# Global filter plus product-key experts on one core: leftover rows in 64 by 64 pieces stacked by DMA, guards from sums of squares, and a new order

## The chip, the cores and the metric

The kernel runs on one core of one Trainium2 chip. The metric is the device time of one execution in microseconds (us). Names of the engines: PE multiplies matrices, DVE is the vector engine, ACT the scalar engine, POOL the GpSimd engine, SP the sync engine, which here only issues transfers.

## The reference, cut to what matters

```python
x: (1, 2048, 576);  xn = layernorm(x)
# spectral part
y = irfft2(rfft2(xn) * (w_r + 1j * w_i))                 # over 2048 and 576
# experts: 32 heads, two halves of 128, 8 keys each
q = einsum("nd,dhc->nhc", xn, w_q)                       # w_q (576, 32, 256)
i1 = argmax(q[..., :128] @ k1.T);  i2 = argmax(q[..., 128:] @ k2.T)
e  = i1 * 8 + i2                                         # one expert per head, gate 1
act = gelu(xn . u[e])                                    # u, v (64, 576)
out = x + y + sum over heads of act * v[e]
```

## The kernel before, in words

The 2048 tokens lie in 16 tiles of 128. Everything is one program whose operations are recorded and then issued in an order that a table of numbers, `ORDER`, writes out by hand; a second table, `BANK`, says which PSUM banks each result takes (`_Plan.issue`, line 305). So every recorded instruction has line 312 in the profile, and groups are told apart by their tiles. Each engine takes its instructions in that order and never passes one by. All transfers are issued by SP, one queue in order. At most eight of them are under way, since their completions turn over eight semaphores.

**Spectral part.** `folds` (509) makes of each token tile the even and odd halves of a row; `dft128` (525) transforms along the sequence in 64-point pieces on halves of PE (64 rows by 128 columns). Of the 161 columns of a half, 128 go into the main store `AB` as an fp16 value and an fp16 remainder, by ACT and DVE. The 33 that are left over go into `ABL`, 99 partitions high: value, value, remainder, stacked. To get them there, `folds` copies the 33 columns three times side by side (`fl`, on ACT or POOL), four matmuls write 99 rows at once, and two evictions (ACT 99 by 256, DVE 33 by 256) end in the right rows. `d_fwd` (785) transforms along the features: per group two matmuls from `ABL`, twelve from `AB`. `s_fwd` (801) and `s_inv` (838) are the second stage along the sequence and its inverse, in fp32 on quarters and halves of PE; `s_mul` (820) between them multiplies with the filter `Wt` (two DVE instructions with results `t`, two on POOL that make `y`). `s_inv` also has four matmuls for the leftover rows, from three copies `yl` that ACT makes. `d_inv` (866) goes back along the features, and `fin` (895) along the sequence. Sixteen groups g pass `d_fwd`, `s_fwd`, `s_mul`, `s_inv`; then sixteen tiles pass `d_inv` and `fin`. The first `d_inv` needs `AB` and `ABL` of all sixteen groups.

**Experts.** `fold_part` (626) reads w_q in 32 loads `w` of 576 KB (five buffers) and multiplies each with differences of the keys (`KP`, four matmuls); the result becomes the matrix `MU` (`fold_end`, `fold_last`). `x_t` (694) loads the transposed tokens `xf` and splits them into `xT`. `scores` (708) multiplies `MU` with `xT` (28 matmuls of 128 by 512 per pair of tiles) and takes maxima over seven differences; `route` (734) turns them into codes with one reduce over seven, and one-hot rows; `combine` (754) sums them into `CAT`. In `fin` eight matmuls per pair of tiles multiply `CAT` with `vS` (fp16 value and remainder of v).

**Guards.** Before a value is split into fp16 it is scaled by its largest magnitude: a maximum per partition, then `allmax` (444): PE transpose, DVE reduce, PE matmul, DVE scaling.

Of the kernel before, what the change touches and what calls it, by code (L numbers as in the profile page):

```python
# [10 lines left out]
F32 = mybir.dt.float32  # L11
# [28 lines left out]
def _consts():  # L40
# [10 lines left out]
    place = [8 * (g % 2) + g // 2 for g in range(16)]  # L51
# [4 lines left out]
    RT = np.concatenate([R.reshape(64, 64).T] * 2)  # L56
# [42 lines left out]
    ev = ll % 2 == 0  # L99
    i = np.arange(127, -1, -1)[:, None]  # L100
    mid = _columns()[:33, None]
    half = np.where(i == 0, 0.5, 1.0)
    C1, S1 = (f(pi2 * (i * ll % 576) / 576) * half for f in (np.cos, np.sin))
    C2, S2 = (f(pi2 * (mid * ll % 576) / 576) for f in (np.cos, np.sin))
# [11 lines left out]
    for b, (m, k) in enumerate(((C1, C2), (S1, S2))):  # L116
        for q, h in enumerate(_hl(_clean(m))):
            dc[:, b, q] = h
        hi, lo = _hl(_clean(k))
        dl[:99, b] = np.concatenate([hi, hi, lo])  # L120
    for b, m in enumerate((_clean(CI) * 64, _clean(SI) * 64)):
        hi, lo = _hl(m)
        for q, h in enumerate((hi, lo)):
            ce = slice(0, 145) if b == 0 else slice(145, 290)
            co = slice(145, 290) if b == 0 else slice(0, 145)
            ic[:, b, q, ce] = h[:128, ce]
            ic[:, b, q, co] = h[161:, co]
        il[:99, b] = np.concatenate([hi[128:161], hi[128:161], lo[128:161]])
# [90 lines left out]
class _Ps:  # L219
# [9 lines left out]
    def rearrange(self, *p, **kw):  # L229
        return _Ps(self.ap.rearrange(*p, **kw), self.tile)  # L230
# [797 lines left out]
```

## Time and profile before

| | us |
|---|---|
| three runs | 207.41, 208.88, 209.98; median 208.88 |
| the profiled execution, its own time | 209.11 |
| its span | 206.3 |
| outside the span | 2.8 |
| PE busy | 195.5 (95%) |
| DVE busy | 172.8 (84%) |
| ACT busy | 120.7 (59%) |
| POOL busy | 97.6 (47%) |
| moved by DMA | 43.39 MB, mean 210 GB/s |

The profile is that of one execution. The chain of waits is followed back from the last instruction. In the timeline a row is a run of like instructions: start, length until the last has ended, engine, operation, output and inputs, tile, count; in square brackets behind it stands how long the engine had been idle and what released it. Since matmuls overlap, the cost of a run of them is the distance between its start and the next row's start. A row of the windows gives the length of a stretch, the busy time of PE, its weight loads, DVE, ACT and POOL with the counts of instructions, then the granted PE clock, the mean busy share of the 16 DMA engines and GB/s.

### The profile page before, as it was taken

How to read it: one execution, taken by the hardware profiler on the slowest of the kernel's cores; microseconds unless marked ns; L12 is line 12 of the kernel's file. 1: busy time of each engine (PE TensorE's matmuls, PEld its weight loads, DVE VectorE, ACT ScalarE, POOL GpSimd, SP SyncE). 2: the span in 40 equal slices, each digit the busy share in tenths (PEclk: the TensorE clock that was granted, in tenths of full speed). 3: DMA queues.
4: the chain of work that ended last, by engine and by line, in shares of the span. 5: the costliest groups of instructions: out<-in, count | busy, mean ns of one | idle time of the engine just before them, and what ended most of it. 6: DMA issues, size and time to landing. Idle time of an engine off the chain costs nothing.

```text
span 206.3 us, 5748 instructions
## 1 busy us (share of the span) xinstructions
PE 195.5 (95%) x2239; PEld 134.3 (65%) x2239; DVE 172.8 (84%) x397; ACT 120.7 (59%) x272; POOL 97.6 (47%) x160
## 2 busy tenths in 40 slices
PE   7588999999998999999999999999999999999992
PEld 2388669786567658544556668565686667868850
DVE  2899898847485787659999999999999999999863
ACT  2799997842437629988686936608682432333400
POOL 4548464002250033179538227405176666959750
PEclk9999999999999999999999999999999999999999
DMA  6999899999999999554725502520000000123195
GB/s 209 394 416 420 308 381 412 403 407 374 376 380 410 335 371 318 176 178 129 280 67 174 211 0 79 165 102 5 0 3 0 0 3 0 62 114 118 65 362 206
DMA packets 14859, 43.39 MB, mean 210 GB/s; under 512 B 1904, under 2 KB 4720, under 8 KB 14576
## 3 DMA queue, kind: packets, MB, share of 16 engines
q1 hardware_dynamic: 14832, 43.03, 56.6%
q8 instruction: 17, 0.28, 0.6%
q14 instruction: 10, 0.08, 0.1%
HBM read 38.30 MB, written 4.72 MB: 209 GB/s over the span
## 4 chain that ended last, share of the span: by engine, by line
PE 84%; DMA 8%; DVE 4%; ACT 1%; issue 1%; POOL 1%; DVEq 0%; SPq 0%; ACTq 0%
PE banks L312 84%; DMA w<-in_wq_dram 6%; DVE A L312 2%; DMA XN<-in_x_dram 1%; DVE st L312 1%; DVE rr L312 1%; ACT t L312 0%; POOL A L312 0%; DVE AB L312 0%; POOL MUL L312 0%; DVE XN L312 0%; ACT rr L312 0%; POOL rr L312 0%; DVEq L1022 0%; ACT yl L312 0%
## 5 line engine op out<-in xcount | busy, mean ns | idle before, releaser
L312 PE MATMUL banks<-MU,xT 128*128 128x512 f16 x192 | 46.3, 379 | 0.0
L312 POOL TENSOR_TENSOR y<-t,t 128x289 f32<-128x289 f32 x32 | 21.5, 695 | 43.8 <-DVE t L312 21.6
L312 PEld LDWEIGHTS <-AB 128*128 128x128 f16 x400 | 33.9, 122 | 6.2 <-issue 1.9
L312 PEld LDWEIGHTS <-xT 128*128 128x128 f16 x224 | 21.3, 100 | 22.8 <-issue 0.9
L312 PE MATMUL banks<-c,AB 128*128 128x145 f16 (+1 forms) x384 | 35.1, 227 | 0.0
L312 POOL TENSOR_TENSOR xT<-xf,xT 128x640 f16<-128x640 f32 x16 | 22.8, 1433 | 24.4 <-DVE w L312 10.4
L312 DVE SCALAR_TENSOR_TENSOR t<-banks,wx,Wt 128x578 f32<-128x578 f32 x32 | 24.4, 812 | 7.1 <-PE banks L312 4.1
L312 POOL TENSOR_TENSOR A<-t 128x289 f32<-128x289 f32 x32 | 21.5, 694 | 7.0 <-DVE MT L312 3.8
L312 DVE TENSOR_TENSOR AB<-banks,AB 128x512 f16<-128x512 f32 x32 | 21.2, 675 | 1.8 <-ACT AB L312 1.7
L312 PE MATMUL banks<-Rs,A 64*128 64x128 f32 x256 | 18.6, 288 | 3.9 <-ACT Rs L312 2.9
L312 ACT ACTIVATE es<-banks,sc 128x290 f32<-128x290 f32 (+1 forms) x16 | 9.9, 625 | 18.9 <-PE banks L312 12.5
L312 PEld LDWEIGHTS banks<-Rs,A 64*128 64x128 f32 x256 | 16.5, 194 | 6.3 <-ACT Rs L312 4.6
L312 PE MATMUL banks<-w,KP 128*32 128x288 f32 x256 | 18.6, 412 | 1.3 <-DMA w<-in_wq_dram 1.2
L312 ACT ACTIVATE AB<-banks 128x512 f16<-128x512 f32 x32 | 18.4, 591 | 1.7 <-PE banks L312 1.2
L312 PE MATMUL banks<-c,ABL 99*128 99x289 f16 (+1 forms) x64 | 18.5, 290 | 0.0
L312 DVE TENSOR_REDUCE MT<-w 128x128 bf16<-128x896 bf16 (+1 forms) x16 | 18.2, 1140 | 0.1
L312 ACT ACTIVATE A<-banks 128x578 f32<-128x578 f32 x16 | 10.3, 645 | 13.1 <-PE banks L312 12.2
L312 PE MATMUL banks<-A,s 64*64 64x289 f32 x256 | 17.8, 410 | 0.0
L312 PE MATMUL banks<-s,y 64*128 64x128 f32 x256 | 17.4, 278 | 0.0
L312 ACT ACTIVATE ABL<-banks 99x256 f16<-99x256 f32 x32 | 11.6, 379 | 9.3 <-PE banks L312 8.8
L312 PEld LDWEIGHTS banks<-s,y 64*128 64x128 f32 x256 | 15.4, 187 | 2.1 <-issue 1.4
L312 DVE SCALAR_TENSOR_TENSOR XN<-banks,sc,XN 128x578 f32<-128x578 f32 (+1 forms) x18 | 12.9, 746 | 1.9 <-PE banks L312 1.9
(124 smaller groups left out, 359.9 us busy)
## 6 DMA issues: line engine op xcount, KB each, us to landing
w<-in_wq_dram SPq DMA_DIRECT2D x32, 576.0 KB, 6.9
xf<-in_xT_dram SPq DMA_DIRECT2D x16, 320.0 KB, 3.3
Wt<-in_W_dram SPq DMA_DIRECT2D x8, 578.0 KB, 6.6
out_dram<-XN SPq DMA_DIRECT2D x14, 288.0 KB, 2.4
s<-in_s_dram SPq DMA_DIRECT2D x16, 192.0 KB, 5.7
XN<-in_x_dram SPq DMA_DIRECT2D x2, 1156.0 KB, 12.6
XN<-in_x_dram SPq DMA_DIRECT2D x3, 578.0 KB, 5.8
c<-in_c_dram SPq DMA_DIRECT2D x1, 868.5 KB, 11.2
```

Of the source, the lines that this page charges most:

```text
L312: o.last = fn(*[x.place() if isinstance(x, _Ps) else x for x in args], **{k: x.place() if isinstance(x, _Ps) else x for k, x in kw.items()})
```

## The change

1. **Leftover rows.** `folds` makes no copies and lays the 33 and the 31 leftover columns next to each other. (Odd halves have 31 that are not zero, so there are 64 in all.) `dft128` multiplies them with one matmul on each half of PE, 65 rows by 64, where there were two. ACT and DVE evict 64 partitions by 128 into a plain store `HL` (a view of a new tile `U`). Once all sixteen tiles are through, a new step `spread` copies `HL` into the stacked `ABL` by six transfers from SBUF to SBUF, 33 or 31 partitions of 4096 bytes each.
2. **The same on the way back.** `s_inv` keeps its eight main matmuls. A new `s_left` handles the leftover rows of two groups at once, by eight matmuls on 64 by 64 quarters; ACT and DVE evict (128 by 256 each), then six transfers of 33 partitions by 4 runs of 128 bytes stack them in `ABL`. The copies `yl` are gone.
3. `d_fwd` and `d_inv` issue the `ABL` matmuls after the `AB` ones, and these may stand apart.
4. **Guards** are roots of sums of squares: ACT squares and sums, one matmul sums over partitions, DVE takes a root by an integer operation on the bits. Ten of eleven `allmax` are replaced (`root`); five large DVE reduces over w_q's fold and two over u and v become six ACT instructions. The ACT squares of the fold write into the last `w` buffer.
5. **Remainder of v** in `fin`: four full matmuls and four on halves, two at a time, instead of eight full ones.
6. **Maximum of the codes** in `route`: three elementwise maxima over halves (2 by 192, 2 by 128, 128 elements) instead of one reduce over 896. The columns of `MU` are ordered for that.
7. **Order.** `place`, `ORDER` and `BANK` are new. Four `xf` loads and the masks `mk` now stand ahead of the last `w` load. There are 157 transfers, 103 before.

The SP queue around the new copies. Before (`w_120` to `w_119` are buffers of the w_q loads, `Wt_113<-in_v` brings v):

```order
L312 DMA c_72<-in_c_dram 128x3474
L312 DMA s_2_116<-in_s_dram 128x384
L312 DMA s_0_114<-in_s_dram 128x384
L312 DMA s_1_115<-in_s_dram 128x384
L312 DMA w_120<-in_wq_dram 128x1152
L312 DMA w_122<-in_wq_dram 128x1152
```

After, `ABL<-U` being the copies of `spread`:

```order
L322 DMA w_120<-in_wq_dram 128x1152
L322 DMA w_116<-in_wq_dram 128x1152
L322 DMA xf_121<-in_xT_dram 128x640
L322 DMA s_1_113<-in_s_dram 128x384
L322 DMA w_117<-in_wq_dram 128x1152
L322 DMA ABL<-U 31x2048
L322 DMA ABL<-U 33x2048
...
L322 DMA w_119<-in_wq_dram 128x1152
L322 DMA w_118<-in_wq_dram 128x1152
L322 DMA w_120<-in_wq_dram 128x1152
```

The 31 and 33 rows come three times in turn. Twelve of the 32 `w` loads stand ahead of the copies, twenty behind them.

PE between the last second-stage step and the first `d_inv`. Before (`s,y` and `s,yl` are `s_inv`, `MU` are scores, `c,ABL` the first `d_inv`):

```order
L312 MATMUL banks<-s_0_114,y_132 128x128 x8
L312 MATMUL banks<-s_0_114,yl_104 99x128 x4
L312 MATMUL banks<-s_1_115,y_133 128x128 x8
L312 MATMUL banks<-s_1_115,yl_105 99x128 x4
L312 MATMUL banks<-s_2_116,y_132 128x128 x8
L312 MATMUL banks<-s_2_116,yl_103 99x128 x4
L312 MATMUL banks<-s_3_117,y_133 128x128 x8
L312 MATMUL banks<-s_3_117,yl_104 99x128 x4
L312 LDWEIGHTS xT_92
L312 MATMUL banks<-MU,xT_92 128x512
...
L312 LDWEIGHTS ABL
L312 MATMUL banks<-c_72,ABL 128x290
```

After (`U` now holds `y`, `id` is a transpose of the experts' coefficients, `c,AB` the first `d_inv`):

```order
L322 MATMUL banks<-s_0_112,U 128x128 x8
L322 MATMUL banks<-s_1_113,U 128x128 x8
L322 MATMUL banks<-s_2_114,U 64x128 x2
...
L322 MATMUL banks<-s_2_114,U 128x128 x8
L322 MATMUL banks<-s_3_115,U 128x128 x8
L322 LDWEIGHTS MT
L322 MATMUL banks<-id_108,MT 128x128
...
L322 LDWEIGHTS AB
L322 MATMUL banks<-c_72,AB 128x145
```

The sixteen score matmuls that stood between the last `s_inv` and the first `d_inv` now stand earlier.

DVE in the same place, after; the four `t` are the last `s_mul`, `lo` the leftover evictions, `AB` the main ones, the others are experts:

```order
L322 SCALAR_TENSOR_TENSOR t_0_104<-banks,wx,Wt_111 128x578
L322 TENSOR_TENSOR lo_130<-banks,lo_130 128x256
L322 TENSOR_REDUCE MT<-w_119 128x32
L322 TENSOR_TENSOR AB<-banks,AB 128x16x32 x2
L322 TENSOR_TENSOR w_120<-w_120,wt 128x896
...
L322 TENSOR_TENSOR w_120<-w_120 128x2x192
L322 TENSOR_TENSOR lo_131<-banks,lo_131 128x256
L322 TENSOR_TENSOR w_120<-w_120 128x2x128
L322 TENSOR_TENSOR AB<-banks,AB 128x16x32
```

One more `AB` eviction follows four small instructions later, and the first `d_inv` waits for it.

The diff's core:

```diff
-    place = [8 * (g % 2) + g // 2 for g in range(16)]
+    place = [4 * (g % 4) + g // 4 for g in range(16)]
...
 ORDER = (
-    19, 20, 21, 22, 0, 25, 26, 11, 27, 30, 31, 23, 426, 28, 14, 39, 29, 3, 32, 33, 40, 42, 47, 46, 8, 2, 1, 4,
+    24, 19, 20, 21, 29, 27, 28, 11, 0, 22, 23, 39, 31, 30, 32, 34, 3, 47, 35, 36, 46, 2, 1, 5, 9, 4, 6, 8, 402,
...
+    def root(src, k, dst, e):
+        p = PS("m", (128, 64))
+        P.matmul(p[:, :k], on[:, 0:1].to_broadcast([128, 128]), src, start=True, stop=True)
+        v = p[:, :k].bitcast(I32)
...
+        V.tensor_scalar(dst.bitcast(I32), v, 0.5, float(0x1FBD1DF5 + (e << 23)), op0=OP.mult, op1=OP.add)
...
     def dft128(t):
-        for b in range(2):
-            for h, r in enumerate(hs):
-                P.matmul(p[:99, h, 256 + 64 * b:320 + 64 * b], fl[r, b], Rs[r, 0], start=True,
-                         stop=True, tile_position=(64 * h, 0))
+        for h, r in enumerate(hs):
+            P.matmul(p[:65, h, 256:320], e[r, 256:321], Rs[r, 0], start=True, stop=True, tile_position=(64 * h, 0))
...
-        A.activation(lo[:99], l[:99], AF.Copy)
-        V.tensor_tensor(lo[:33], l[:33], lo[:33], op=OP.subtract)
+        A.activation(lh, l, AF.Copy)
+        V.tensor_tensor(ll, l, lh, op=OP.subtract)
+
+    @staged
+    def spread():
+        for k, q in enumerate((0, 0, 1)):
+            for b, n in enumerate((33, 31)):
+                Q.dma_start(ABL[n * k:n * k + n, b], HL[31 * (1 - b):31 * (1 - b) + n, q])
...
     def fold_part(b, s):
-            if (b, s) == (3, 3):
-                V.tensor_reduce(mm_[:, 3 + h:4 + h], mt[b][:, h, :288], axis=AX, op=OP.max, apply_absolute_value=True)
...
+            A.activation(w[:, 0:2], mt[b][:, :, :288], AF.Square, accum_out=mm_[:, b:b + 1])
...
     def route(r):
-        V.tensor_reduce(v0, wv, axis=AX, op=OP.max)
+        V.tensor_tensor(wv[:, :, 4:7], wv[:, :, 4:7], wv[:, :, 0:3], op=OP.max)
+        V.tensor_tensor(wv[:, :, 3:5], wv[:, :, 3:5], wv[:, :, 5:7], op=OP.max)
+        V.tensor_tensor(v0.rearrange("p (t m) -> p t m", t=2), wv[:, :, 3], wv[:, :, 4], op=OP.max)
...
+    @staged
+    def s_left(g):
+        p = PS("c")
+        for ri in range(2):
+            for q in range(2):
+                y, s = Y[g + q], S32[g + q][:, 192:]
+                for e in range(2):
+                    r, o = slice(64 * e, 64 * e + 64), 64 * (e ^ q)
+                    P.matmul(p[o:o + 64, q, :128], y[r, ri, 128:192], s[r, 64 * ri:64 * ri + 128], start=(ri == 0),
+                             stop=(ri == 1), tile_position=(64 * e, o))
...
+        A.activation(hi, pv, AF.Copy)
+        V.tensor_tensor(lo, pv, hi, op=OP.subtract)
+        for k, n in enumerate((0, 0, 1)):
+            for e in range(2):
+                to = ABL[33 * k:33 * k + 33].rearrange("p b (a e n) -> p (b a) e n", a=2, e=2)
+                Q.dma_start(to[:, :, e, 32 * g:32 * g + 64], h[64 * e:64 * e + 33, n])
...
     def fin(t, ys):
+        for h in range(2):
+            for i in range(2):
+                r = slice(64 * i, 64 * i + 64)
+                P.matmul(ps[i][:, h, :L], CAT[r, t + i, :], vS[r, 1, L * h:L * h + L], start=False, stop=False,
+                         tile_position=(64 * i, 0))
...
-                for q in range(2):
-                    P.matmul(ps[i][:, h, :L], CAT[:, t + i, :], vS[:, q, L * h:L * h + L], start=False, stop=(q == 1))
+                P.matmul(ps[i][:, h, :L], CAT[:, t + i, :], vS[:, 0, L * h:L * h + L], start=False, stop=True)
...
     dft128(15)
+    spread()
```

More of the change, by code (lines that the diff above doesn't have):

```diff
@@ L101, in _consts @@
     mid = _columns()[:33, None]
-    half = np.where(i == 0, 0.5, 1.0)
-    C1, S1 = (f(pi2 * (i * ll % 576) / 576) * half for f in (np.cos, np.sin))
-    C2, S2 = (f(pi2 * (mid * ll % 576) / 576) for f in (np.cos, np.sin))
+    C1 = np.cos(pi2 * (i * ll % 576) / 576) * np.where(i == 0, 0.5, 1.0)
+    S1 = np.sin(pi2 * ((i + 1) * ll % 576) / 576)
+    C2, S2 = np.cos(pi2 * (mid * ll % 576) / 576), np.sin(pi2 * (mid[:31] * ll % 576) / 576)
     eps = np.where((ll == 0) | (ll == 288), 1.0, 2.0)[:, None]
@@ L270, in __init__ @@
     def __init__(self, nc):
-        self.ops, self.stage, self.pack, self.made, self.tiles = [], 0, set(), 0, []
+        self.names = {}
+        self.ops, self.stage, self.pack, self.made, self.tiles, self.split = [], 0, set(), 0, [], False
         self.engines = [_Engine(self, n, getattr(nc, n)) for n in ("vector", "scalar", "gpsimd", "tensor", "sync")]
@@ L289, in add @@
         last = self.ops[-1] if self.ops else None
-        if (eng == "tensor" and last is not None and last.eng == eng and last.stage == self.stage
+        if (eng == "tensor" and last is not None and last.eng == eng and not self.split and last.stage == self.stage
                 and last.cols + cols < 2160 and (last.tiles == tiles or last.tiles | tiles <= self.pack)):
@@ L303, in add, with cut @@
             v.users.add(len(self.ops) - 1)
+    def cut(self):
+        self.split = True
     def issue(self, tc):
@@ L403, in _body @@
     ABL = K([128, 2, S], F16, "ABL")
+    U = K([128, 2316], F32, "U")
+    slots["y"], slots["es"] = ([U[:, 579 * i:579 * i + 578] for i in range(4)], [U[:, 580 * i:580 * i + 580] for i in range(2)])
+    turn["y"] = turn["es"] = 0
+    HL = view(U, [64, 2, S], F16)
     ABg = AB.rearrange("p q c (g n) -> p q c g n", g=16)
     ABLg = ABL.rearrange("p b (g n) -> p b g n", g=16)
-    place = [8 * (g % 2) + g // 2 for g in range(16)]
+    place = [4 * (g % 4) + g // 4 for g in range(16)]
     ABt = AB.rearrange("p q c (n t) -> p q c n t", t=16)
     ABLt = ABL.rearrange("p b (n t) -> p b n t", t=16)
-    ABi = AB.rearrange("p q c (a g e m) -> p q (c a) g e m", a=2, g=16, e=2)
-    ABLi = ABL.rearrange("p b (a g e m) -> p (b a) g e m", a=2, g=16, e=2)
+    ABi = AB.rearrange("p q c (a e g m) -> p q (c a) g e m", a=2, g=16, e=2)
     wu = AB[:, 0, 0, 0:512]
@@ L439, in g @@
             plan.stage += 1
+            plan.names[plan.stage] = (f.__name__, *(x for x in args if isinstance(x, int)))
             return f(*args)
@@ L563, in uv_prep @@
         Q.dma_start(vs, a["v2"])
-        V.tensor_reduce(uv[:, 0:1], uf, axis=AX, op=OP.max, apply_absolute_value=True)
-        V.tensor_reduce(uv[:, 1:2], vs, axis=AX, op=OP.max, apply_absolute_value=True)
-        allmax(uv[:, 0:2], 2, sc[:, 0:2])
+        for k, z in enumerate((uf, vs)):
+            A.activation(vS[:, 0, :z.shape[1]], z, AF.Square, accum_out=uv[:, k:k + 1])
+        root(uv[:, 0:2], 2, sc[:, 0:2], 1)
+        V.tensor_scalar(sc[:, 0:2], sc[:, 0:2], 1e-10, None, op0=OP.max)
         V.reciprocal(sc[:, 4:6], sc[:, 0:2])
@@ L787, in d_fwd @@
         for b in range(2):
-            P.matmul(p[:, b, :L], ABLg[:99, b, place[g], :], dl[:99, b, :], start=True, stop=False)
             for c in range(2):
@@ L791, in d_fwd @@
                 for n, (ha, hb) in enumerate(((0, 0), (0, 1), (1, 0))):
-                    P.matmul(p[:, b, cs], ABg[:, ha, 2 * b + c, place[g], :], dc[:, b, hb, cs], start=False,
-                             stop=(c == 1 and n == 2))
+                    P.matmul(p[:, b, cs], ABg[:, ha, 2 * b + c, place[g], :], dc[:, b, hb, cs], start=(c == n == 0), stop=False)
+        plan.cut()
+        for b in range(2):
+            P.matmul(p[:, b, :L], ABLg[:(99, 93)[b], b, place[g], :], dl[:(99, 93)[b], b, :], start=False, stop=True)
         t = T([128, 2, L], F32, "A2", 4)
@@ L840, in s_inv @@
         p = PS("c", (128, 2, 4, 128))
-        (y, yl), s = Y.pop(g), S32.pop(g)[:, 192:]
-        for c in range(3):
+        y, s = Y[g], S32[g][:, 192:]
+        for c in range(2):
             for ri in range(2):
@@ L868, in d_inv @@
         for b in range(2):
-            P.matmul(p[:, b, :290], ABLt[:99, b, :, t], il[:99, b, :], start=True, stop=False)
             for c in range(2):
@@ L872, in d_inv @@
                 for n, (ha, hb) in enumerate(((0, 0), (0, 1), (1, 0))):
-                    P.matmul(p[:, b, cs], ABt[:, ha, 2 * c + b, :, t], ic[:, b, hb, cs], start=False,
-                             stop=(c == 1 and n == 2))
+                    P.matmul(p[:, b, cs], ABt[:, ha, 2 * c + b, :, t], ic[:, b, hb, cs], start=(c == n == 0), stop=False)
+        plan.cut()
+        for b in range(2):
+            P.matmul(p[:, b, :290], ABLt[:99, b, :, t], il[:99, b, :], start=False, stop=True)
         eo = T([128, 2, L], F32, "eo2", 2, "t1")
@@ L959, in _body @@
         s_inv(g)
+        if g % 2:
+            s_left(g - 1)
         if g + 2 < 16:
```

115 lines of the change are left out of this document (55 added, 60 removed), and 125 rows, old and new, of tables (BANK, ORDER).

## The prediction

> **What bounds the kernel now.** I read the page first, then the chain of waits, then the stretches of 5 us, then PE's and DVE's timelines.
>
> ```profile
> PE 195.5 (95%) x2239; PEld 134.3 (65%) x2239; DVE 172.8 (84%) x397; ACT 120.7 (59%) x272; POOL 97.6 (47%) x160
> PE   7588999999998999999999999999999999999992
> DVE  2899898847485787659999999999999999999863
> DMA  6999899999999999554725502520000000123195
> GB/s 209 394 416 420 308 381 412 403 407 374 376 380 410 335 371 318 176 178 129 280 67 174 211 0 79 165 102 5 0 3 0 0 3 0 62 114 118 65 362 206
> ```
> ```profile
> 22.65 6.62 DMA w<-in_wq_dram
> 29.32 27.28 PE banks L312 x407
> 56.61 6.03 DMA w<-in_wq_dram
> 62.68 139.31 PE banks L312 x1438
> 202.01 0.52 DVE XN L312
> ```
>
> The page shows PE full nearly everywhere. In the first 16 slices (up to 82 us) DMA is full too; from slice 19 on DVE is. The chain is PE for 139.31 us, and ahead of that it goes through `w` loads twice. So there are two stages: until the last piece of w_q has landed PE and DMA both bind, and afterwards PE with DVE close behind.
>
> ```profile
> 20.00:25.00 5.00, 4.81 (x80) 3.03 (x76) 4.40 (x14) 4.92 (x16) 2.74 (x8) 1.00 0.88 305
> 30.00:32.00 2.00, 2.00 (x38) 2.00 (x38) 1.85 (x9) 1.85 (x7) 0.05 (x1) 1.00 1.04 422
> 32.00:34.00 2.00, 2.00 (x40) 2.00 (x38) 1.55 (x4) 1.68 (x6) 1.75 (x4) 1.00 1.01 412
> 110.00:115.00 5.00, 5.00 (x42) 2.92 (x39) 4.97 (x8) 3.66 (x8) 4.15 (x6) 1.00 0.72 228
> w<-in_wq_dram SPq DMA_DIRECT2D x32, 576.0 KB, 6.9
> L312 ACT ACTIVATE AB<-banks 128x512 f16<-128x512 f32 x32 | 18.4, 591 | 1.7 <-PE banks L312 1.2 <-DVE ABL L312 0.4
> ```
>
> A full DMA moves 412 GB/s on 16 engines, 25.75 GB/s on each; the one early dip (305) cost 5 x (1 - 305/412) = 1.3 us. At 110 us PE and DVE are both at 5 of 5, and DMA has room.
>
> ```profile
> 41.27 0.29 PE L312 MATMUL banks<-c,ABL 99*128 99x289 f16 x1
> 76.79 1.18 PE L312 MATMUL banks<-w,KP 128*32 128x288 f32 x16
> 77.90 0.30 PE L312 MATMUL banks<-c,ABL 99*128 99x289 f16 x1
> 80.83 1.16 PE L312 MATMUL banks<-s,y 64*128 64x128 f32 x16
> 81.83 0.60 PE L312 MATMUL banks<-s,yl 64*99 64x128 f32 x8
> 82.27 1.06 PE L312 MATMUL banks<-s,y 64*128 64x128 f32 x16
> 83.16 0.60 PE L312 MATMUL banks<-s,yl 64*99 64x128 f32 x8
> 83.86 1.03 PE L312 MATMUL banks<-MU,xT 128*128 128x512 f16 x4
> 87.65 2.18 PE L312 MATMUL banks<-A,s 64*64 64x289 f32 x32
> 89.77 2.33 PE L312 MATMUL banks<-MU,xT 128*128 128x512 f16 x10
> ```
>
> The last use of a `w` ends at 77.90 and the scores begin at 83.86. I sum the change up to that first score matmul, then from it to the end (118.1 us, to 202.0).
>
> **Up to the first score: DMA.** Counting the transfers ahead of the last `w` load gives 28.09 MB before and 30.30 MB after: four `xf` (1.31 MB), `mk` (.05), four copies of `s_left` (.07), and the six of `spread` (.79). By bytes alone that is 2.21/.412 = +5.4 us. But bytes are the price only if a transfer is shared by all 16 engines, and here lies the doubtful cost. All transfers of the profile have 128 partitions, 8 for each of 16 engines. The new ones have 33 and 31. No row shows such a shape. Its price has two ends. Shared evenly, 31 rows of 4096 bytes (127 KB) take 127/412 = .3 us. On one engine alone they take 127/25.75 = 4.9 us, three of them 14.8 us, and whatever comes behind on that engine comes later by that. I take the upper end: if the shares are equal and of whole rows, as 128 rows over 16 engines allow, then 31, a prime, leaves one engine, and 33 leaves eleven with three rows each (.48 us a copy). Every later `w` load has a sixteenth of its bytes on the crowded engine and is complete only when that has landed.
>
> The Trainium skill ("DMA: Bandwidth & Descriptors", section "Why a DMA increments its semaphore by 16 and not by 1") says the same of transfers issued in hardware: the engine count is the largest number up to 16 that divides the slowest dimension on both sides, with 127 partitions as an example of one engine. By that rule the sum is the one for the upper end below; no run here shows it yet.
>
> The crowded engine then has (30.30 - .79 - .07)/16 + 3 x .127 + 3 x .012 + .006 = 2.26 MB ahead of the last `w`, against 28.09/16 = 1.755 before: .509 MB, /25.75 = +19.8 us. Against it stand lost times that a queue never empty does not have: the dip of 1.3, and behind the copies (about 41 us, 15.3 MB) up to 12.8 MB/.412 = 31.0 against 77.1 - 41.3 = 35.8 us, so up to 4.8 (the first eight slices of the GB/s row make 15.2 MB in 41.3 us; the last load lands between 76.79 and 77.90, say 77.1). Behind the last `w` use the new order puts one `s_left` (.5 by the `s,yl` row), one `d_fwd` (1.03), a root, transposes (.5, .3) and an `s_fwd` (2.12 by 87.65 to 89.77), 4.9 us with the root at .25, where 6.0 stood: -1.1. Sum +12.6 to +18.7; I take **+15**. Shared evenly the same sum is 5.4 - 1.3 - 1.1 = +3.0 down to -1.8; I would take +1.6, since loads behind the copies still wait for the same five buffers.
>
> The copies also wait in SP's queue for the last leftover eviction of ACT and DVE, with twenty `w` loads behind them. The 15.3 MB ahead last until about 41 us, and before the first use of finished `ABL` stood at 41.27, so I price that wait at nothing; each us by which it comes later is lost one to one. The four ACT squares of the fold hold a `w` buffer some .6 us longer each (591 ns for a like size); queued loads hide that, 2.4 us if not.
>
> What PE saves in this stage changes nothing then: half of the leftover work,
>
> ```profile
> 17.23 0.52 PE L312 MATMUL banks<-Rs,yl 64*99 64x64 f32 x8
> 17.73 2.18 PE L312 MATMUL banks<-Rs,A 64*128 64x128 f32 x32
> ```
>
> (.50 us for two tiles, so 16 x .125 = 2.0), three pairs of leftovers on the way back (1.3) and some .5 of guards, less the `s_fwd` of 2.1: 1.7 us that lie under the loads. So do DVE's reduces over the fold.
>
> **From the first score to the end: PE.** One `s_fwd` now lies ahead of the scores: -2.1. Leftovers of five pairs: the `s,yl` row costs 82.27 - 81.83 = .44 per two rows of four matmuls, .88 a pair; quarters, four at a time, halve it: 5 x .4 = -2.0. Remainder of v:
>
> ```profile
> 172.30 1.21 PE L312 MATMUL banks<-A,c 64*64 64x289 f32 x16
> 173.44 1.16 PE L312 MATMUL banks<-vS,MT 128*128 128x289 f16 x8
> 174.44 0.29 PE L312 MATMUL banks<-c,ABL 99*128 99x290 f16 x1
> 84.72 0.27 PE L312 MATMUL banks<-c,wm 128*1 128x128 f32 x1
> ```
>
> eight `vS` take 1.00 us; four of them two at a time save a quarter, 8 x .25 = -2.0. Five roots save the transpose and one matmul less, some .12 each: -.6. Together **-6.8** (nothing of it if DVE becomes the bound there).
>
> For quarters between other shapes the first `s,y` row stands for a price: 81.83 - 80.83 = 1.00 behind other work, 83.16 - 82.27 = .89 behind its kind, .1 more for a change of shape. The Trainium skill ("TensorEngine Tiling (Array Packing)", section "Key Properties") says that a change of tiling mode drains the engine; the row agrees with a tenth of a us, and for eight `s_left` the sum would be .8 us worse. I leave that in the range.
>
> **The hand-over.** The new order has no score matmuls left between the last `s_fwd` and the first `d_inv`. PE has two `s_left` (.5 each), four `s_inv` (3.8) and a transpose (.5): 5.3 us. DVE has in that place, in order, four `t`, two leftover evictions, one long reduce, four `AB`, and small steps:
>
> ```profile
> 122.35 3.00 DVE L312 SCALAR_TENSOR_TENSOR t<-banks,wx,Wt 128x578 f32<-128x578 f32 x4
> L312 DVE TENSOR_TENSOR AB<-banks,AB 128x512 f16<-128x512 f32 x32 | 21.2, 675 | 1.8 <-ACT AB L312 1.7
> L312 DVE TENSOR_TENSOR ABL<-banks,ABL 33x256 f16<-33x256 f32 x32 | 12.5, 406 | 1.5 <-ACT AB L312 0.8 <-ACT ABL L312 0.5
> L312 DVE TENSOR_REDUCE MT<-w 128x32 f32<-128x1024 bf16 x8 | 9.6, 1205 | 0.0
> L312 DVE TENSOR_REDUCE MT<-w 128x128 bf16<-128x896 bf16 x8 | 8.6, 1076 | 0.1
> L312 DVE TENSOR_TENSOR w<-w,MT 128x512 bf16<-128x512 bf16 x16 | 6.5, 416 | 0.1
> L312 DVE TENSOR_TENSOR w<-w,wt 128x896 bf16<-128x896 bf16 x8 | 5.3, 660 | 0.1
> out_dram<-XN SPq DMA_DIRECT2D x2, 144.5 KB, 1.9
> ```
>
> 3.00 + 2 x .41 + 1.2 + 4 x .675 + .66 + some 1.5 of small ones = 9.9 us, so PE waits 4 to 5 us. The last leftovers must also be issued six times by SP and land (1.9 us for the nearest transfer). I take **+5**, with ends 0 (DVE done early) and +7. The three-step maximum lies here: by the slope from 512 to 896 elements (.416, .660), 384, 256 and 128 elements cost .335, .254, .172, together .76 against 1.076; if each step cost what 512 do, 1.25. Eight times -.3 or +.2 on DVE is in those ends.
>
> **Sum**, against the profiled execution, 209.11 us (span 206.3 and 2.8 around it): +15 - 6.8 + 5 = +13.2, 222.3 us. It lay .2 above the median, so I forecast **222.1 us**; its own range is 214.5 (12.6 - 6.8 + 0) to 227.
>
> **Rivals.** *Shared evenly, wait at the hand-over:* the copies spread over all engines and cost bytes only: +1.6 - 6.8 + 5 = -.2, **208.7 us**. For it speaks that every transfer so far kept 16 engines busy (share 1.04 at 30 us); against it, that 31 and 33 rows have no sixteenth. *Shared evenly, no wait at the hand-over*, the other side: DVE reaches the hand-over early because it idles in the first stage (slices 9 to 16 show 4 to 8 tenths), so that PE finds `AB` written: +1.6 - 6.8 = -5.2, **203.7 us**, down to 200.5 if the stage loses nothing at all. Against it speaks that DVE runs at 4.97 of 5 at 110 us and at nine tenths all the way there. It decides as soon as DVE is ahead of PE by 4 us at the last `s_fwd`.
>
> **How the numbers follow.** One engine for 31 rows has .73, even shares with the wait .15, even shares without it .12. A measurement of this kernel tells about 2%, 204.7 to 213.1 us, from no change. The first case lies above but for .02, the second within, the third below but for .02: faster .10, within .19, slower .71. The range leaves out the third case and the topmost of the first: **206 to 227**.
>
> **What would show it.** In the profile after: the three copies of 31 rows land 5 us apart while 33 rows land earlier; the DMA share falls far under 1 between 41 and 95 us although loads are queued; PE waits some 10 us at its first `ABL` matmul, and then for `w` loads that land 1.4 us apart (576 KB/16 on one engine); the first score stands near 99 us. PE from there to the end takes 116 us with one wait of 5 us before the first `d_inv`. The forecast is wrong if those copies land within 3 us of their issue, with the DMA share near 1: then the first score stands at 82 to 87 us and the rivals are left.

## The result, and the profile after

The changed kernel takes **247.99 us** (median of four runs, 247.21 to 250.3) against 209.14 before: a ratio of 1.189, interval 1.177 to 1.200. The forecast was 222.1 and its range ended at 227. The direction was right, the size was not: +39 us where +13 was expected.

The page of the changed kernel, engines and slices:

```profile
span 248.5 us, 5683 instructions
PE 203.2 (82%) x2165; PEld 132.9 (54%) x2165; DVE 167.6 (67%) x391; ACT 124.7 (50%) x261; POOL 95.7 (39%) x161
PE   7569989600698989496999999999999853999992
PEclk9995999975599999869799999999999995899998
DMA  6996999485428999954064630054113010010666
```

PE, full before, now has a hole of two slices at 47 to 64 us and smaller ones at 103 and 205. The granted clock, .999 on the mean before and .915 now, falls at five places. DMA has dips at 23, at 43 to 50 and at 56 to 73 us. PE's timeline of the changed kernel at these places:

```profile
46.86 0.94 PE L322 MATMUL banks<-c,AB 128*128 128x145 f16 x12
64.52 1.61 PE L322 MATMUL banks<-c,ABL 99*128 99x289 f16 x6 [16.73 <-DMA ABL<-U]
104.73 0.90 PE L322 MATMUL banks<-c,xT 128*128 128x128 f32 x3 [3.36 <-DVE MU L322]
120.53 0.49 PE L322 MATMUL banks<-MU,xT 128*128 128x512 f16 x1
204.09 0.88 PE L322 MATMUL banks<-c,AB 128*128 128x145 f16 x10 [1.58 <-DVE AB L322]
208.76 0.68 PE L322 MATMUL banks<-c,ABL 99*128 99x290 f16 x2 [3.79 <-DMA ABL<-lo]
243.59 1.80 DVE L322 SCALAR_TENSOR_TENSOR XN<-banks,sc,XN 128x289 f32<-128x289 f32 x4 [0.42 <-PE banks L322]
```

The first score stands at 120.53 (83.86 before, 99 expected): +36.7 where the sum had +15. From there to the last result (243.59) are 123.1 us (118.1 before, 116.3 expected): +5.0 where the sum had -1.8. So both halves missed, the first by 22 us.

The changed kernel in windows (the last three columns are granted clock, DMA share, GB/s):

```profile
17.00:19.00 2.00, 1.66 (x24) 1.53 (x24) 1.57 (x7) 2.00 (x8) 1.88 (x6) 0.84 1.02 422
19.00:23.00 4.00, 4.00 (x40) 4.00 (x40) 3.67 (x11) 3.16 (x9) 3.02 (x11) 0.50 0.90 366
56.00:58.00 2.00, 0.00 (x0) 0.00 (x0) 0.00 (x0) 0.00 (x0) 0.00 (x0) 0.50 0.06 23
62.00:64.00 2.00, 0.00 (x0) 0.00 (x0) 0.00 (x0) 0.00 (x0) 0.00 (x0) 0.50 0.07 26
71.00:73.00 2.00, 2.00 (x30) 0.70 (x26) 1.20 (x2) 0.26 (x1) 0.00 (x0) 1.00 0.06 22
104.00:107.00 3.00, 2.27 (x15) 1.10 (x19) 1.69 (x2) 3.00 (x4) 0.00 (x0) 0.50 1.04 363
```

Two things are to be seen. At 56 to 58, 62 to 64 and 71 to 73 us the share is .06 or .07, a sixteenth, at 22 to 26 GB/s, which fits one DMA engine at work and fifteen idle, at the 25.75 GB/s of the sum. And the clock is at .50 behind five waits or groups of waits of PE (those that end at 16.90, 64.52, 104.73, 116.77 and 208.76), also when PE is full again (4.00 of 4 at 19 to 23). It is not so behind every wait: behind one of 1.05 us that ends at 90.65 it stays at 1.00.

SP's timeline and the groups by shape of the changed kernel:

```profile
41.76 5.15 SPq L322 DMA_DIRECT2D ABL<-U  x6
189.65 17.66 SPq L322 DMA_DIRECT2D ABL<-lo  x18
```
```profile
L322 DVE SCALAR_TENSOR_TENSOR MU<-banks,sc,MU 128x336 f16<-128x336 f32 x4 | 6.7, 1762 | 4.8 <-ACT MU L322 4.8
L322 ACT ACTIVATE MU<-banks,sc 128x336 f16<-128x336 f32 x4 | 6.5, 1895 | 0.0
```

SP needs .86 us for each of the first copies (5.15/6, with the pauses between them), and for the last eighteen 17.66 us. And the evictions into `MU`, which the prediction did not look at, take 1.9 and 1.8 us each. For the kernel before, by shape:

```profile
L312 ACT ACTIVATE MU<-banks,sc 128x336 f16<-128x336 f32 x4 | 2.1, 539 | 5.1 <-PE banks L312 3.9 <-DVE sc L312 1.3
L312 DVE SCALAR_TENSOR_TENSOR MU<-banks,sc,MU 128x336 f16<-128x336 f32 x4 | 2.2, 563 | 0.7 <-ACT MU L312 0.7
```

The new order of `MU`'s columns, made for the maximum in three steps, has them write seven 16-bit values in turn that lie 128 bytes apart; in the kernel before the seven are neighbours.

### The profile page after: what moved, and what is told of

Its sections match the earlier page's. It is cut to its first block, busy times and chain, and to the rows that moved or that the text cites. A ratio compares the mean times of both kernels' runs of the same rounds, so it can differ in the third digit from the quotient of the medians.

```text
span 248.5 us, 5683 instructions
## 1 busy us (share of the span) xinstructions
PE 203.2 (82%) x2165; PEld 132.9 (54%) x2165; DVE 167.6 (67%) x391; ACT 124.7 (50%) x261; POOL 95.7 (39%) x161
## 4 chain that ended last, share of the span: by engine, by line
PE 60%; DMA 16%; DVE 13%; ACT 6%; issue 2%; SPq 1%; POOL 1%; DVEq 0%; ACTq 0%
PE banks L322 60%; DMA ABL<-U 7%; DMA w<-in_wq_dram 6%; ACT MU L322 2%; DVE t L322 2%; DVE AB L322 2%; DMA XN<-in_x_dram 2%; DVE MU L322 1%; SPq L322 1%; DVE st L322 1%; DVE w L322 1%; DVE A L322 1%; DVE MT L322 1%; ACT AB L322 1%; DMA ABL<-lo 1%
## 5 line engine op out<-in xcount | busy, mean ns | idle before, releaser
L322 POOL TENSOR_TENSOR U<-t,t 128x289 f32<-128x289 f32 x32 | 21.9, 702 | 57.2 <-DVE mm__95 L322 34.8
L322 PE MATMUL banks<-c,ABL 99*128 99x289 f16 (+1 forms) x64 | 13.8, 318 | 20.5 <-DMA ABL<-U 16.7
L322 PE MATMUL banks<-Rs,A 64*128 64x128 f32 (+1 forms) x320 | 22.0, 291 | 6.2 <-DVE rr L322 2.4
L322 ACT ACTIVATE A<-banks 128x578 f32<-128x578 f32 x16 | 10.1, 647 | 32.0 <-PE banks L322 31.9
L322 PE MATMUL banks<-s,U 64*128 64x128 f32 (+1 forms) x384 | 24.5, 287 | 1.9 <-DVE t L322 1.0
L322 PEld LDWEIGHTS banks<-Rs,A 64*128 64x128 f32 (+1 forms) x320 | 20.6, 197 | 9.2 <-ACT Rs L322 5.6
L322 PEld LDWEIGHTS banks<-s,U 64*128 64x128 f32 (+1 forms) x384 | 20.2, 174 | 8.3 <-issue 4.3
L322 ACT ACTIVATE U<-banks,sc 128x580 f32<-128x580 f32 (+1 forms) x16 | 9.7, 623 | 21.8 <-PE banks L322 21.4
L322 DVE SCALAR_TENSOR_TENSOR t<-banks,sc,U 128x290 f32<-128x290 f32 (+1 forms) x24 | 11.8, 541 | 11.3 <-ACT U L322 8.8
L322 POOL TENSOR_TENSOR A<-XN 128x256 f32<-128x256 f32 (+1 forms) x32 | 13.5, 444 | 14.0 <-DVE A L322 4.7
L322 PEld LDWEIGHTS <-ABL 99*128 99x128 f16 x64 | 6.7, 130 | 22.3 <-issue 21.7
```

What stands on the lines that cost most here:

```text
L322: o.last = fn(*[x.place() if isinstance(x, _Ps) else x for x in args], **{k: x.place() if isinstance(x, _Ps) else x for k, x in kw.items()})
```

## The experiments

Theories to be told apart: **one engine** (31 rows land on one DMA engine), **evictions** (scattered writes into `MU`), **issue** (SP's time per copy), **clock** (the half clock behind waits). Each run is paired with the kernel before on the same chip, 208.2 to 209.2 us. The first two experiments and the two with the suspected copy alone are one execution each; executions of the changed kernel differ by 3 us (247.21 to 250.3).

**Copies of 31 rows in two, of 16 and 15.**

```diff
-                Q.dma_start(ABL[n * k:n * k + n, b], HL[o:o + n, q])
+                m = (33, 16)[b]
+                Q.dma_start(ABL[n * k:n * k + m, b], HL[o:o + m, q])
+                if b: Q.dma_start(ABL[n * k + m:n * k + n, b], HL[o + m:o + n, q])
```

> The changed kernel, but each copy of 31 rows is issued as one of 16 rows and one of 15; nothing else differs. Theory (a copy lies on as many engines as divide its rows, so 31 rows lie on one): PE's wait for ABL behind 47 us falls from 16.7 us to 2 to 6 us (nine issues of .8 us and a landing of 2 us stay), no stretch is left in which the DMA share is .06 there, and the time falls by 10 to 16 us to 232 to 238 us. Rival (copies from SBUF to SBUF are slow by their bytes, or PE waits for SP's issuing): the wait stays above 12 us and the time above 244 us.

236.08 us, 12 less. The wait at the first `ABL` matmul:

```profile
51.06 1.02 PE L322 MATMUL banks<-c,ABL 99*128 99x289 f16 x6 [3.60 <-DMA ABL<-U]
```

From 16.73 to 3.60. The theory of one engine holds, and 27 of the 39 us stay.

**Evictions in the order of MU's columns.** The same values go to the same places, only the instruction walks 48 neighbours first and seven columns last.

```diff
-        m = (...)[:, :, :448].rearrange("p h (e m) -> p h m e", e=7)[:, :, 0:48]
+        m = (...)[:, :, :448].rearrange("p h (e m) -> p h e m", e=7)[:, :, :, 0:48]
+        pv = p.rearrange("p b m e -> p (b m) e")[:, :, :7].rearrange("p m e -> p e m")
```

> The changed kernel, but the evictions into MU and MUL walk through the same elements in another order: the 48 or 16 neighbouring columns innermost instead of the seven differences that lie 128 bytes apart in the new column order. Theory (the scattered two-byte writes made these evictions slow, 1.9 us where .54 stood): ACT's 128x336 evictions take .5 to .7 us, DVE's likewise, the first score comes 8 to 13 us earlier than 121.2 us, and the time falls to 235 to 240 us. Rival (they are slow because ACT and DVE read the same PSUM banks as PE writes, or because PE waits for the copies alone): the evictions stay above 1.4 us and the time at 246 to 250 us.

239.43 us, 8.6 less. Groups by shape of this kernel:

```profile
L322 ACT ACTIVATE MU<-banks,sc 128x336 f16<-128x336 f32 x4 | 1.9, 546 | 0.0
L322 DVE SCALAR_TENSOR_TENSOR MU<-banks,sc,MU 128x336 f16<-128x336 f32 x4 | 2.2, 563 | 1.4 <-ACT MU L322 1.4
```

From 1895 and 1762 ns to 546 and 563. It is the walk that costs, not the layout.

**Both edits.**

> The changed kernel with both edits. If the two causes add up, 248 falls by 10 to 16 and by 8 to 13 us to 219 to 230 us. If each only uncovers the other (the copies hide the evictions' delay or the other way round), the time stays above 232 us. Against the kernel before (209 us) it stays slower by 5 to 10%, since SP's issue of each stacked copy at .83 us still holds the hand-over.

224.77 us (222.14 to 228.49), ratio 1.074 (1.064 to 1.085): 23.2 less than the change, the two singly 20.5. They add up. That this lies near the forecast of 222.1 is luck: the crowded engine was in the forecast and is gone here.

**The suspected copy alone.** In the kernel before, three copies from `XN` into `MU`, which is empty then, issued where `spread` stands; they have nothing to do with the result. The second run has 32 k + 32 as the end of the rows, 32 in place of 31.

```diff
+    for k in range(3):
+        r = slice(32 * k, 32 * k + 31)
+        Q.dma_start(MU[r, 0]...bitcast(F32), XN[r]...[:, 0:1024])
```

> The kernel before, with three copies of 31 rows of 4096 bytes from SBUF to SBUF (from x's store into a part of MU that is written later) issued behind the twelfth w load; nothing needs them. Theory (one engine takes all 31 rows): that engine gets 3 x 127 KB = 14.8 us at 25.75 GB/s more, every later w load completes later, the first score stands 10 to 17 us after 83.9 us and the time is 218 to 228 us. Rival (copies cost by bytes or by their issue): 209 to 212 us.

> The same with 32 rows in place of 31, which 16 engines can share, two rows each. Theory: 3 x 131 KB over 16 engines are .9 us and three issues some 2 us, so the time is 208 to 212 us, although more bytes are moved than with 31 rows. Rival (any copy from SBUF to SBUF into few partitions is slow): the same 218 to 228 us as with 31 rows.

225.13 and 211.71 us: +16.8 and +3.4. One row more in each, and the copies are cheaper by 13.4 us. PE's waits with 31, then with 32 rows:

```profile
PE banks L312 <- DMA c<-in_c_dram: 15.8, 1, 15.8
```
```profile
PE banks L312 <- DMA c<-in_c_dram: 1.5, 1, 1.5
```

The kernel before has no such wait. It is for a load of 128 rows behind the copies, which fits a sixteenth of it lying on the crowded engine.

**Repeated matmuls against the half clock**, on top of both edits: at four places where PE waits, an operation is issued 2 to 20 more times.

```diff
+FILL = {111: 4, 295: 14, 612: 2, 889: 20}
-            for fn, args, kw in o.calls:
+            for fn, args, kw in o.calls * (1 + FILL.get(i, 0)):
```

> The kernel of e3 with matmuls that are repeated, with the same result, in four places where PE waits: near 16 us (two small ones, four times more), ahead of the wait for ABL (a sum of squares, 14 times more, 3.6 us), near 75 us (eight, twice more) and ahead of the first inverse step (two transposes, 20 times more). Theory (PE's granted clock falls to half after a stretch of some 3 us in which PE is busy under half the time, and costs half of the next 5 to 9 us): the half-clock stretches behind 18, 51, 78 and 207 us go, and the time falls by 5 to 10 us from 222 to 225 us to 213 to 219 us. Rival (the clock falls for another reason, such as power or DMA, or the extra matmuls cost as much as they save): the clock rows keep their dips, 222 to 230 us.

224.2 us (221.24 to 224.44, and one of 256.54), ratio 1.070 (1.061 to 1.079), against 224.77: not the 5 to 10 us that were expected. The clock without the repeats (in the version of the next experiment, which differs from both edits at the hand-over alone), then with them:

```profile
PEclk9996799996999999999999999999999987999997
```
```profile
PEclk9999999999999999999999999999999975999999
```

The dips ahead of 180 us are gone, and in the profiled executions the first score stands at 92.42 in place of 97.41. The median does not follow. From the first score to the last result it takes 125.3 us here, against 122.8 to 123.5 in the changed kernel and the versions so far: the repeats at the hand-over take time themselves, and the wait there grows:

```profile
173.54 2.52 PE L323 MATMUL banks<-id,MT 128*128 128x128 f16 x42
181.94 0.68 PE L323 MATMUL banks<-c,ABL 99*128 99x290 f16 x2 [4.83 <-DMA ABL<-lo]
```

**Three of the last six copies issued by ACT**, on top of both edits.

```diff
-                Q.dma_start(to[:, :, e, ...], h[64 * e:64 * e + 33, n])
+                (A if g == 14 and e else Q).dma_start(to[:, :, e, ...], h[64 * e:64 * e + 33, n])
```

> The kernel of e3 with three of the last pair's six stacked copies issued by ACT instead of SP. Theory (the last wait for ABL, 3.7 us, is SP's issuing at .83 us a copy): the wait falls by 3 x .83 = 2.5 us to 1 to 1.5 us, the time by 2 to 3 us to 219.5 to 222.5 us. Rival (the wait is the landing, or the queue's backlog of transfers): the wait stays above 3 us and the time within 1 us of that of e3.

221.47 us (220.33 to 223.48), ratio 1.060 (1.054 to 1.065): 3.3 less, where 2 to 3 were expected. The executions of the two versions overlap, so the wait, .30 where 3.79 stood in the changed kernel, shows it better than the time. The hand-over:

```profile
182.97 0.68 PE L322 MATMUL banks<-c,ABL 99*128 99x290 f16 x2 [0.30 <-issue]
```

**The copies of `spread` whole, issued by POOL**, on top of that; the second run adds the repeats at 111.

```diff
+                plan.ops[-1].calls = [(nc.gpsimd.dma_start, *plan.ops[-1].calls[0][1:])]
```

> The kernel of e7, but the six copies of spread are issued by POOL, whole (33 and 31 rows), and no longer by SP. Theory (besides the engine that 31 rows crowd, nine issues of .8 us held SP from 41 to 49 us, so that DMA stood half idle and w loads came late): SP goes on with w loads, DMA's share stays above .8 from 41 to 51 us, the first score comes 3 to 6 us earlier and the time is 215 to 219 us against 221.5 us of e7. Rivals: copies issued by POOL crowd one engine as SP's did, then PE waits over 10 us for ABL and the time is 230 us or more; or issuing was never in the way, 220 to 223 us.

> The kernel of e8 with the one early repeat of e6 (two small matmuls near 16 us, four times more, 1 us of PE). Theory (the clock's half stretch from 18 to 26 us costs PE some 4 us and starts because PE is busy under half of the time from 15 to 18 us): the clock row shows no dip there, the DFT ends 3 us earlier, and the time falls by 1 to 4 us against e8. Rival (DMA, not PE, sets the first score by then): the dip goes, the first score stays within 1 us of that of e8.

227.01 and 224.52 us: 5.5 and 3.1 more. POOL issues all six in 3.27 us and no engine stands alone, but PE waits longer:

```profile
54.95 1.61 PE L322 MATMUL banks<-c,ABL 99*128 99x289 f16 x6 [7.01 <-DMA ABL<-U]
```
```profile
42.00:50.00 8.00, 5.94 (x80) 4.28 (x79) 3.21 (x13) 4.06 (x8) 3.27 (x6) 1.00 1.00 313
50.00:58.00 8.00, 3.05 (x19) 2.53 (x20) 0.00 (x0) 1.97 (x4) 0.00 (x0) 0.60 1.02 326
58.00:62.00 4.00, 4.00 (x56) 2.29 (x54) 0.45 (x1) 0.65 (x1) 0.00 (x0) 0.94 0.09 35
```

SP now goes on with `w` loads, and the copies share the engines with them (share 1.00). PE, waiting, frees no `w` buffer, so DMA runs dry behind it (.09). The early repeat moves the first score from 100.43 to 98.21 and the median by 2.5 us, within the 1 to 4 that were expected; the intervals of the two ratios overlap (1.079 to 1.093 and 1.072 to 1.082).

**Remainder of v on halves, alone, in the kernel before.**

```diff
+                    P.matmul(ps[i][:, h, :L], CAT[r, t + i, :], vS[r, 1, L * h:L * h + L], ..., tile_position=(64 * i, 0))
```

> The kernel before with one part of the change alone: the remainder of v on halves, two at a time. Theory (PE sets the end there, eight pairs of tiles save a quarter of 1.00 us each): 1.5 to 2 us faster, 206.3 to 207 us against 208.3 us, ratio .990 to .994. Rival (DVE's last steps set the end, or the halves cost as much as full matmuls): ratio .997 to 1.003.

208.74 us (12 runs) against 208.5 (17 runs): ratio 1.0017 (.9988 to 1.0045). Nothing. This kernel in the windows of the last stage:

```profile
160.00:170.00 10.00, 10.00 (x79) 6.38 (x78) 9.79 (x21) 4.29 (x11) 6.58 (x11) 1.00 0.01 2
180.00:190.00 10.00, 9.96 (x127) 6.88 (x125) 9.94 (x22) 3.71 (x7) 7.57 (x13) 1.00 0.32 120
```

The block of `vS` shrank from 1.00 to .87 us, not by a quarter, so eight of them save 1.0 us and not 2.0. Why not even that arrives is not shown. DVE (the fourth figure that is not in brackets) is at 9.79 and 9.94 of 10, before at 9.79 and 9.76, and is the likely bound; but no wait of PE for DVE shows here, PE is at 10.00 and 9.96.

**Issue on ACT and repeats in the first stage together; then the 31-row copies of `spread` issued by ACT as well.**

```diff
+FILL = {111: 4, 295: 14, 612: 2}
...
-                Q.dma_start(ABL[n * k:n * k + m, b], HL[o:o + m, q])
+                (A if b else Q).dma_start(ABL[n * k:n * k + m, b], HL[o:o + m, q])
```

> The copies of 31 rows in two, contiguous evictions and three issues on ACT, as in the version of 221.5 us, and besides it eighteen groups of repeated matmuls in the first stage (the same as before without those at the hand-over), which add PE work of no effect. Clock theory: the half clock in the first stage costs time that counts; with the hand-over no longer waiting for SP's issues, the first score's gain of some 5 us (97.4 to about 92.5) comes through to the end: 215 to 218.5 us. Rival, the clock only fills what the loads would make PE wait for anyway: the first score moves, but the time stays at 219.5 to 223 because DVE sets what follows.

> The same with the six copies of the 31 leftover rows of spread (three of 16 and three of 15 rows) issued by ACT, in its own queue, so that SP issues three copies ahead of the next w load and not nine. Issue theory: nine issues of .83 us hold SP for 7.5 us while the DMA engines stand half idle (share .47 at 45 to 50 us); six fewer give back 5 us of SP, of which 2 to 4 us reach the first score: 2 to 4 us less than the run beside it. Rival, as with POOL's queue: the copies then stand behind w loads on the same engines and PE waits at its first ABL matmul: no gain or up to 4 us more.

220.81 us (ratio 1.057, 1.048 to 1.066) and 230.28 us. By its median the first is not distinguishable from the 221.47 without repeats. In the profiled executions the first score stands at 93.15 in place of 97.41, and the last result comes as much earlier (212.32 in place of 216.94); but the one without repeats was the longest of its four (223.48), so what the repeats are worth stays open. The second is 9.5 us worse. With three copies on SP and six on ACT the `w` loads come forward, and PE waits at its first matmul on the 93 rows that the copies of ACT bring:

```profile
54.50 1.37 PE L323 MATMUL banks<-c,ABL 93*128 93x289 f16 x5 [4.26 <-DMA w<-in_wq_dram]
```

The profile puts this wait down to a `w` load, but the matmul reads none; it reads those copies, the last of which ACT issued as late as 48.5 us.

**What is left: bytes, or SP held?** On top of the version of 220.81: four `xf` loads and their splits behind the last `w` load; a `w` load behind each three copies of `spread`; both.

```diff
-    ... 325, 269, 268, 273, 270, 271, 272, ... 329, 327, 331, ...
+    ... 325, 269, 268, 329, 273, 270, 327, 271, 272, 331, ...
```

> The version with the copies in two, contiguous evictions, three issues on ACT and repeated matmuls (220.8 us, first score at 93.15 in its profile), with the four xf loads and their splits behind the last w load again: 1.31 MB less ahead of it. Bytes theory: DMA is full on both sides of the copies, so the last w load lands 1.31/.412 = 3.2 us earlier, the first score stands near 90 to 91.5 and the time is 2 to 3 us less, 217.5 to 219. Rival, the time ahead of the last w load is SP's hold and not bytes: the loads shift, the last w load and the first score do not (92.5 to 94), 220 to 223 us.

> The same version with the nine copies of spread in three groups, and one of the next three w loads behind each group, so that SP issues a w load every 2.5 us instead of none for 7. Hold theory: the DMA rate of 40 to 50 us, now 169 and 251 GB/s, comes near 350, the first score stands 2 to 4 us earlier (89 to 91) and the time is 217 to 219 us. Rival: SP waits at those loads for a free buffer, the last copies land later and PE waits at its first ABL matmul: first score 93 or later, 220.5 to 224 us.

> Both edits of the two runs beside it. If bytes and hold are both paid at full price, 215 to 217 us with the first score at 87 to 88.5; if one only, as that run alone; if neither, 220 to 223 us, and what is left of the distance to the kernel before lies elsewhere than in the transfers ahead of the last w load.

240.42, 225.9 and 243.07 us: all worse. The first doesn't tell: ACT's splits, moved along, stood ahead of evictions that PE needs, so that PE waited 10.9 us for ACT; the third has a like wait (10.1). In the second the rate at 40 to 50 us rises from 169 and 251 to 240 and 259 GB/s, and PE waits for the copies again, 3.55 us (none in the 220.81), then for `w`:

```profile
51.37 1.63 PE L325 MATMUL banks<-c,ABL 99*128 99x289 f16 x6 [3.55 <-DMA ABL<-U]
73.50 1.18 PE L325 MATMUL banks<-w,KP 128*32 128x288 f32 x16 [1.60 <-DMA w<-in_wq_dram]
```

The four `xf` once more, with ACT's splits behind its last evictions of the second stage:

> As e13, but ACT's splits of the four xf now stand behind its last evictions for the second stage, so that ACT no longer waits for loads that come last. Bytes theory: 1.31 MB less ahead of the last w load, the last use of a w 3 us earlier than at 87.67 (84 to 85.5), and the time 217.5 to 219.5 if ACT's 3.3 us of splits in the gap ahead of the first score do not eat it. Rival, bytes ahead of the last w are not what binds: the last use of a w stays at 87 to 88 us and the time at 220 to 224.

229.8 us: PE now waits 4.50 us at its first score for `MU`, which ACT evicts behind the splits. But the question has its answer in two rows, the last use of a `w` without the move and with it:

```profile
87.67 0.69 PE L323 MATMUL banks<-w,KP 128*32 128x288 f32 x8 [0.33 <-DMA w<-in_wq_dram]
```
```profile
87.62 0.69 PE L325 MATMUL banks<-w,KP 128*32 128x288 f32 x8 [0.56 <-DMA w<-in_wq_dram]
```

1.31 MB less ahead of it (3.2 us at full rate) and it stands where it stood. What SP waited for most between 40 and 90 us in the version of 220.81:

```profile
SPq L323 <- PE banks L323: 14.5, 10, 5.3
```

The loads there wait for buffers that PE frees; PE sets their pace, not bytes. (This version has the repeats in it, 3.5 us of PE's time up to the first score, so it does not settle the same for the changed kernel.)

## Why the prediction was wrong, point by point

**The copies on one engine: right in cause and size, not in the path.** The sum priced one engine over even shares at 15 - 1.6 = 13.4 us; the two runs with the suspected copy differ by 13.4, and splitting the copies gave 12. (To the tenth this is chance, with one execution each.) The shares of .06 and .07 show the one engine. The Trainium skill ("DMA: Bandwidth & Descriptors", section "Why a DMA increments its semaphore by 16 and not by 1") had the same rule; the trace agrees, at 22 to 26 GB/s.

But the forecast saw a queue that is never empty, some 10 us of waiting at the first `ABL` matmul, and then waits for `w` loads. PE waited 16.73 us there and 1.8 for `w` up to the first score, and the queue did stop: the next transfers were not issued until copies had landed. SP's waits for that in the changed kernel, then in the kernel before with 31 and with 32 rows:

```profile
SPq L322 <- DMA ABL<-U: 11.3, 3, 5.5
```
```profile
SPq L312 <- DMA MU<-XN: 8.6, 2, 5.1
```
```profile
SPq L312 <- DMA MU<-XN: 0.2, 1, 0.2
```

This fits the limit of eight transfers under way: a copy that takes 5 us on its one engine then also holds back the loads for the other fifteen.

**The new columns of MU: the step that failed.** "The three-step maximum lies here" priced part 6 by its maxima alone. These were right (353, 286 and 221 ns, .86 together against .76 predicted and 1.076 before). But the other end of the same edit, the walk of the evictions, was costed at nothing, and costs 8.6 us (11.3 when the copies are split as well, 236.08 - 224.77). With the walk alone mended the first score stands at 109.33 in place of 120.53; 99 was forecast, so this step is half of what the first part missed. It is not all: 239.43 us, the time with the walk alone mended, still lies 12 us above the range, and the steps that follow were mis-sized too. The evictions stand one behind the other on the chain of waits of the changed kernel:

```profile
99.55 1.67 ACT MU L322
101.31 1.63 ACT MU L322
102.97 1.72 DVE MU L322
...
111.64 1.64 ACT MUL L322
114.62 1.74 DVE MUL L322
117.01 1.78 ACT MU L322 x3
```

PE waits behind the third for 3.36 us, and the scores stand behind the rest.

**"issued six times by SP and land (1.9 us for the nearest transfer)": mis-sized.** The hand-over's waits for DVE and ACT (.70, .29, .72, .48 and 1.58) make 3.8 us, close to the 4 to 5 of the forecast. The copies add 3.79, for which the +5 left 1 us at most: 7.6 us together, above the upper end of 7. An issue is .83 us, where a DRAM load's is about .4, and the copies are issued one after the other; with three issues on ACT 3.3 us go.

**"What PE saves in this stage changes nothing" and the bytes: wrong.** The sum took the loads for the bound of the first stage and charged 5.4 us for 2.2 MB. The last comparison shows, for the version with repeats, that 1.3 of these 2.2 MB cost nothing where PE sets the pace. What PE loses there counts: up to the first score, for the kernel before and for the one of 221.47 us,

```profile
sum 83.86, PE 77.18 PEld 57.30 DVE 62.09 ACT 56.73 POOL 29.73; mean PE 15.44 PEld 11.46 DVE 12.42 ACT 11.35 POOL 5.95
```
```profile
sum 97.41, PE 82.32 PEld 57.83 DVE 57.89 ACT 61.93 POOL 32.18; mean PE 16.46 PEld 11.57 DVE 11.58 ACT 12.39 POOL 6.44
```

PE is busy 5.1 us longer (some 2.8 for the `s_fwd` that moved ahead, 9.7 against 6.9 us in the groups by shape; the rest would fit the half clock, but no run shows it) and idle 15.1 us in place of 6.7, of which 3.7 for the copies and 2.5 for DVE's `rr` ahead of the first transform, a wait that the kernel before does not have.

**The clock, not foreseen.** The sum took full speed throughout; the mean granted clock was .915. The Trainium skill ("TensorE: Matmul & The Clock Gate", section "HAM oscillation — how this bites in real kernels") warns that a gap on PE of over some 3.4 us halves its clock; the trace agrees, with the clock at .50 behind the waits of 16.73 and 3.79 us, and adds that a wait of 1.65 us did it too, with PE busy .35 of the 2 us around it, although PE was busy 1.66 of the next 2. 40 matmuls took 4.32 us there; the same 40 at 9.04, at full clock, took 2.58. Keeping PE busy removes the dips; how much that pays was not shown (220.81 against 221.47, and 224.52 against 227.01), the repeats having their own price (3.5 us of `wm` matmuls against .3).

**From the first score on: some half of the -6.8 seen.** With the issue wait gone this stretch is 119.5 us (216.94 - 97.41), 118.1 before. 5.0 us of it are waits at the hand-over, which the kernel before does not have, so the rest became 3.6 us shorter (2.6 in the changed kernel, 123.1 - 7.6 against 118.1). For one part of the -6.8, the remainder of v, -2.0 was forecast and nothing measured. This fits the sum's own proviso, "nothing of it if DVE becomes the bound there", but does not prove it.

**The rivals** with even shares fell with the first profile. Small slips in the working change nothing: the steps behind the last `w` use make 4.7 and not 4.9 us, the savings from the first score on 6.7 and not 6.8, and the stated ends give 214.7 and 227.8 where 214.5 and 227 stand. **Open:** the 12 to 13 us between the best versions of the change (220.81 and 221.47) and the kernel before are accounted for by rows (PE busy and idle, above, for the 221.47), not by runs that take each away; in particular how much of it is the half clock. No version tried beats the kernel before.

## What to carry to other kernels

When a layout is changed for one reader, price every writer of it, by the walk of its last dimension. A copy between SBUF rows that SP issues is priced by how its rows divide over the DMA engines, and by the issuer's time, before its bytes; and a queue ahead of it is part of its price: three ways of not holding SP (POOL, ACT, `w` loads in between) all put the copies into the stream of loads and cost 5 to 9.5 us. A saving on a full engine is not yet a saving of time where the next engine is nearly full too: the halves alone saved 1.0 us of PE's blocks and nothing in time.

## What the runs showed of the hardware that was not expected

- A 16-bit eviction of 128 by 336 from PSUM takes 546 (ACT) and 563 ns (DVE) when it writes neighbours, 1895 and 1762 when seven values in turn lie 128 bytes apart.
- Issuing a copy of 33 partitions from SBUF to SBUF in runs of 128 bytes holds SP .83 us, one of 31 or 33 rows of 4096 bytes .79 (median of six); a load of 128 rows from DRAM .33 to .47. POOL took .51 (median) for each of the latter copies.
- Three copies of 127 KB (31 rows) from SBUF to SBUF cost the kernel before 16.8 us, three of 131 KB (32 rows) 3.4, in one execution each.
- PE's granted clock was .50 for 4 us and more behind a gap of 1.65 us (16.90), when PE had also been little busy before; behind one of 1.05 us (90.65) it stayed at 1.00.
